# A tail ordered by hand, and DMA transposes for the last three steps, in a retention kernel with a gated output block

## The chip, the cores and the metric

The kernel runs on one core of one Trainium2 chip. The metric is the device time of one execution in microseconds (us); all inputs start in the chip's memory (HBM) and the result ends there. Five engines work side by side, each with its own in-order queue of instructions: TensorE (PE in the profile; PEld are its weight loads), VectorE (DVE), ScalarE (ACT), GpSimd (POOL) and SyncE (SP), which here only issues DMAs.

## The reference

Eight batches, eight heads, 576 positions, 64 elements per head. First retention: scores with a decay that depends on the head, kept on and below the diagonal, times the values. Its output, with the heads side by side as 512 channels, goes through a gated block: a causal convolution of five taps for every channel gives a gate, a matrix product gives a value, and the product of both goes through a second matrix.

```python
scores = scale * np.matmul(q, k.transpose(0, 1, 3, 2))      # 8 x 8 x 576 x 576
ret = scores * Dmat                                         # gamma[h] ** (i - j) for i >= j, else 0
x = np.matmul(ret, v)                                       # then heads side by side: 8 x 576 x 512
for kk in range(5):
    gate_pre += conv_w[kk] * xp[:, kk:kk + S, :]            # xp: x with four zero rows ahead
gate = 1.0 / (1.0 + np.exp(-gate_pre))
out = (gate * (x @ w_val)) @ w_out
```

## The kernel before

**Steps.** The 576 positions of a batch are two chunks of 256 and a rest of 64. The list `steps` (L82 to L91) has 20 steps. Sixteen are full ones, one for each batch and chunk, in the order of the batches. Four are rest steps, each with the rests of a pair of batches on the two halves of the partitions; `REMD` (L63) says how many steps after its pair each rest step is put. In the kernel before the rest steps are numbers 6, 9, 16 and 19. The loop over the steps is at L630.

**What a step does.** `load` (L94) issues DMAs of keys, queries and values in float32 on SP, four steps ahead. `cast` (L222) scales them by the decay and writes bfloat16 tiles `kb`, `qb`, `vb` on GpSimd, two steps ahead. `transp` (L245) turns `kb` and `qb` on TensorE, 128x128 at a time, into the PSUM tiles `tpk` and `tpq`; ACT copies the first to `kt` (L263), VectorE the second to `qt` (L265). `state` and `state_sum` (L296, L311) carry the sum over earlier positions, `inter` (L332) multiplies the queries by it, `scores` (L269) forms the scores (PE L282) and masks them on VectorE into `am` (L289), `values` (L346) multiplies them by the values (PE L357), and `evac` (L359) copies the result `o` into the transposed activations `xt` (or `xr` for the rests), one half on VectorE and one on ACT.

**The order.** The order within a step is written by hand as lists of short names: `FULL[0]` and `FULL[1]` for the first and second chunk, `PART` for a rest step (L627 to L629). `Sa`, `Sb` and `Sr` are scores, `T` is `transp` of the next step, `X` and `XS` the state of the next step, `I` is `inter`, `Va`, `Vb`, `Vr` are values, `E` is `evac`, and `B` pushes a block of the gated part into the list `work`. A number such as `4.45` calls `fill` (L604), which takes pieces of work from that list while a credit in us lasts. `Q` and `G` pull single convolution taps.

**The gated part** comes in 12 blocks, of 256 or 512 positions (`push_block`, L423). Block 8 is batch 6 (512 positions), blocks 9 and 10 are the two chunks of batch 7, block 11 is the rests of the last four batches; these three have 256 positions each. A block has four channel groups d = 0 to 3 of 128 channels. Its pieces are:

- `conv` of two groups on TensorE: five taps as products with diagonal matrices (PE L439, tile `cps`, 40 matmuls), then two sigmoids on ACT (L445, tile `gt`).
- For the blocks in `DV` (L67: 8 to 11) the groups 2 and 3 are not on TensorE. Group 2 is five products on ACT (L459) added on GpSimd (L461), group 3 is five multiply-adds on VectorE (L463, L465). Their sigmoids are in `gate` (L468), called from `val`.
- `val` (L480): four matmuls by the value matrix into `vps` (PE L487), then gate times value on VectorE into `zt` (L489).
- `outp` (L493): four matmuls by the output matrix into `ops` for 128 positions (PE L496), a copy to `ob` on ACT (L499), and a store on SP (L505).

**PSUM** has eight slots in three pools: `glp` 4, `scp` 2, `opp` 2. After the last step, `tail` is set (L697) and `gps` (L406) gives out slots of `scp` and `opp` in turn, two each. Then the rest of `work` is emptied in its order. At that point it holds the second half of block 7's `outp`, then blocks 8 to 11; the first `outp` of a block comes after the next block's `conv`.

Of the kernel before, what the change touches and what calls it, by code (L numbers as in the profile page):

```python
# [14 lines left out]
F32 = mybir.dt.float32  # L15
# [16 lines left out]
def kernel(  # L32
# [10 lines left out]
    nc = tc.nc  # L43
# [178 lines left out]
    def cast(s):  # L222
        u, bb, n = steps[s]
        r = st[s]
        R = 1 if bb is None else 2
        shp = [P, R, H, D]
        f0 = n * 2
        nb = 2 if bb is None else 4
        kb = cs.tile(shp, BF16, tag=f"kb{R}", name="kb", bufs=nb)
        qb = cs.tile(shp, BF16, tag=f"qb{R}", name="qb", bufs=nb)  # L230
        vb = cs.tile(shp, BF16, tag=f"vb{R}", name="vb", bufs=nb)

        how = C1 if s == 1 else "PP" + VC[s % len(VC)]
        for e, dst, src, f in ((how[0], kb, r["kf"], fk), (how[1], qb, r["qf"], fq)):
            (nc.vector if e == "D" else nc.gpsimd).tensor_tensor(  # L235
                dst, src.rearrange("p h r d -> p r h d"),
                f[:, f0:f0 + R, :].unsqueeze(3).to_broadcast(shp), op=ALU.mult)
        vsrc = r["vf"].rearrange("p h r d -> p r h d")
        if how[2] == "A":
            nc.scalar.copy(vb, vsrc)  # L240
        else:
            nc.gpsimd.tensor_copy(vb, vsrc)  # L242
        r.update(qb=qb, kb=kb, vb=vb)

    def transp(s, which="kq"):  # L245
        if s >= NS:
            return
        r = st[s]
        R = 1 if steps[s][1] is None else 2
        for nm in which:  # L250
            src = r[nm + "b"]
            tp = (scp if TPS else glp).tile([P, HP, R, P], BF16, tag="sc" if TPS else "gps", name="tp" + nm)
            for hp in range(HP):
                for rr in range(R):
                    nc.tensor.transpose(tp[:, hp, rr, :],  # L255
                                        src[:, rr, 2 * hp:2 * hp + 2, :].rearrange("p a d -> p (a d)"), ident)
# [145 lines left out]
    tail = [None]  # L402

    def gps(shape, name):

        pools = [(glp, "gps")] if tail[0] is None else [(scp, "sc"), (opp, "o")]  # L406
        if tail[0] is not None:
            tail[0] += 1
        pool, tag = pools[(tail[0] or 0) // 2 % len(pools)]
        return pool.tile(shape, F32, tag=tag, name=name)  # L410

    def push_block(xt, bi, t0, segs):
# [37 lines left out]
        def tap(d, kk):  # L450
# [13 lines left out]
            else:  # L464
                nc.vector.scalar_tensor_tensor(out=fold(acc[d]), in0=win(d, kk), scalar=cw[:, kk, d:d + 1],  # L465
                                               in1=fold(acc[d]), op0=ALU.mult, op1=ALU.add)

        def gate(d):  # L468
            while pend[me, d]:
                pend[me, d].pop(0)()  # L470
            gt = gl.tile([P, DM], F32, name="gt")[:, 0:N]
            if d == 2:
                nc.scalar.activation(gt, acc[d], AF.Sigmoid)
            else:
                for y in range(2):
                    nc.scalar.activation(gt[HS[y]], acc[d][HS[1 - y]], AF.Sigmoid)
            g[d] = gt
            gated.add((me, d))

        def val(d):  # L480
            if onv and d in (1, 2):
                gate(d + 1)
            if d == 0:
# [5 lines left out]
            nc.vector.tensor_tensor(z[0][:, d, 0:N], g[d], vp, op=ALU.mult)  # L489
            if tail[0] is not None and d in PULL:  # L490
                pull(2 if d < 3 else 3, KC)

        def outp(m):  # L493
            op = gps([P, DM], "ops")
            for d in range(DT):
                nc.tensor.matmul(op, lhsT=z[0][:, d, m * P:(m + 1) * P], rhs=wout[:, d, :],  # L496
                                 start=(d == 0), stop=(d == DT - 1))
            ob = os_.tile([P, DM], F32, name="ob")
            nc.scalar.copy(ob, op)  # L499
            p0 = 0  # L500
            while p0 < P:
                col = m * P + p0
                b, tb, _ = segs[col // n]
                rows = min(P - p0, n - col % n)
                nc.sync.dma_start(out=out[b, tb + col % n:tb + col % n + rows, :], in_=ob[p0:p0 + rows])  # L505
                p0 += rows

        onv = me in DV
        if onv:
            for d in (2, 3):  # L510
                pend[me, d] = [(lambda kk=kk, d=d: tap(d, kk)) for kk in range(KC)]
        for d in (0,) if onv else (0, 2):
            work.append((conv, d, 0.15 + 2.15 * N / 512))
        work.extend(late)
# [22 lines left out]
    def first(op, hv, e):  # L537
# [56 lines left out]
        elif op == "E":  # L594
            xts[0] = xtb[0]
            for x in range(2):
                copy(e[x], xtb[0][:, ps, 0, PAD + x * P:PAD + (x + 1) * P].rearrange("p a (i r) -> p a r i", r=2),
                     r["o", hv][x].rearrange("p a (r i) -> p a r i", r=2))

    LOOK = 4  # L600
    credit = [0.0]
    usable = ["conv0"]
# [27 lines left out]
    for s in range(NS):  # L630
        u, bb, n = steps[s]
        last = u == B // 2 - 1
        if s + LOOK < NS:
            load(s + LOOK)
        if s > 1 and s + 2 < NS:
            cast(s + 2)
        for op in (PART if bb is None else FIRST if s == 0 else SECOND if s == 1 else FULL[n]):
            if op[:2] in ("D0", "D2"):
# [59 lines left out]
    while work or late:  # L698
        if not work:
            work.extend(late)  # L700
            late.clear()
        fill(1.0)


# [28 lines left out]
```

## Time and profile before

| | us |
|---|---|
| median of 8 runs | 183.52 (182.56 to 185.64) |
| the profiled execution, its time | 183.68 |
| its span, from the first to the last instruction | 181.9 |
| busy in it: PE, DVE, ACT, POOL | 158.8, 123.0, 105.9, 104.2 |
| last load issued (rest step 19), its last part | 123.9 |
| last copy to `ob` ends | 177.72 |

A time in the trace counts from the start of the span. The profiled execution took 1.78 us more than its span. The chain of waits follows the work that ended last back from the last instruction; each of its lines has the start, the time, the engine, the tile, the line in the kernel and the number of instructions. The timeline has the start, the time, the engine, the line, the operation, what it writes and reads with shapes, and in brackets the idle time before it and what ended it.

### The profile page before, as it was taken

What the parts mean: (1) busy time and instruction counts of PE and PEld (TensorE: products, weight loads), DVE (VectorE), ACT (ScalarE), POOL (GpSimd) and SP (SyncE); (2) the same over time, 40 slices, a digit from 0 to 9 for tenths busy, and PEclk for the clock granted to TensorE, in tenths of its full rate; (3) what the DMA queues carried; (4) which work ended last, traced back from release to release, by engine and by line L of the source; (5) the groups of instructions that cost most, each with busy time, mean ns of one, the idle gap of its engine ahead of it and who ended that gap; (6) DMA issues with size and microseconds to landing.
All of it is one profiled execution on the core that took longest, in us unless ns stands there. A gap on an engine that the chain in (4) does not pass through costs nothing.

```text
span 181.9 us, 7690 instructions
## 1 busy us (share of the span) xinstructions
PE 158.8 (87%) x3345; PEld 105.3 (58%) x3345; DVE 123.0 (68%) x233; ACT 105.9 (58%) x214; POOL 104.2 (57%) x101
## 2 busy tenths in 40 slices
PE   0579879958999998999988999989999989999970
PEld 0357556746666565566755597775677534556630
DVE  2969573769669456865498769649679880658830
ACT  6754757454642755175544766554587324989860
POOL 5059199987476966498929761992307600145420
PEclk9999999999999999999999999999999999999998
DMA  5999999999999999999999999986140005032334
GB/s 158 279 302 384 304 278 294 294 302 234 279 308 276 191 298 361 260 293 294 356 286 291 219 281 305 280 252 146 52 182 9 0 4 231 4 141 90 119 117 115
DMA packets 69039, 40.35 MB, mean 222 GB/s; under 512 B 14202, under 2 KB 63374, under 8 KB 69006
## 3 DMA queue, kind: packets, MB, share of 16 engines
q1 hardware_dynamic: 68976, 39.85, 77.7%
q8 instruction: 26, 0.43, 1.0%
q14 instruction: 7, 0.06, 0.1%
q10 hardware_dynamic: 30, 0.01, 0.0%
HBM read 30.42 MB, written 9.44 MB: 219 GB/s over the span
## 4 chain that ended last, share of the span: by engine, by line
PE 65%; DVE 14%; ACT 11%; issue 4%; POOL 2%; POOLq 0%; ACTq 0%; DVEq 0%
PE cps L439 16%; PE ops L496 16%; PE vps L487 12%; DVE am L289 5%; PE o L357 4%; PE tpk L255 4%; PE sc L282 4%; ACT gt L445 3%; PE tpq L255 3%; DVE accs L465 3%; PE o L344 2%; POOL accs L461 2%; PE ds L306 2%; DVE zt L489 2%; ACT kt L263 2%
## 5 line engine op out<-in xcount | busy, mean ns | idle before, releaser
L235 POOL TENSOR_TENSOR kb<-kf,fk 128x1024 bf16<-128x1024 f32 (+1 forms) x19 | 32.8, 1725 | 36.0 <-DMA kf<-in_k_dram 32.3
L289 DVE TENSOR_TENSOR am<-sc,mask_c 128x512 bf16<-128x512 f32 x64 | 40.9, 680 | 4.6 <-PE sc L282 4.5
L439 PE MATMUL cps<-xt,diag 64*64 64x512 bf16 (+1 forms) x680 | 36.6, 348 | 1.1 <-ACT xt L263 0.9
L496 PE MATMUL ops<-wout,zt 128*128 128x512 bf16 x144 | 34.4, 380 | 0.9 <-DVE zt L489 0.7
L489 DVE TENSOR_TENSOR zt<-gt,vps 128x256 bf16<-128x256 f32 (+1 forms) x48 | 25.6, 550 | 13.7 <-PE vps L487 11.1
L439 PEld LDWEIGHTS <-diag 64*64 64x64 bf16 x800 | 27.1, 109 | 9.9 <-issue 2.9
L235 POOL TENSOR_TENSOR qb<-qf,fq 128x1024 bf16<-128x1024 f32 (+1 forms) x19 | 32.7, 1720 | 0.2
L487 PE MATMUL vps<-xt,wval 128*128 128x512 bf16 (+1 forms) x160 | 31.0, 337 | 0.6 <-ACT xt L263 0.4
L461 POOL TENSOR_TENSOR accs<-accs,prod 128x256 f32<-128x256 f32 (+1 forms) x16 | 15.1, 942 | 28.6 <-ACT prod L459 27.7
L445 ACT ACTIVATE gt<-cps 128x512 f32<-128x512 f32 (+1 forms) x40 | 17.8, 496 | 20.1 <-PE cps L439 20.1
L499 ACT COPY ob<-ops 128x512 f32<-128x512 f32 x36 | 20.7, 586 | 11.3 <-PE ops L496 9.9
L487 PEld LDWEIGHTS <-wval 128*128 128x128 bf16 x192 | 17.8, 97 | 13.7 <-issue 1.9
L263 ACT COPY kt<-tpk 128x1024 bf16<-128x1024 bf16 (+1 forms) x19 | 17.5, 923 | 9.2 <-PE tpk L255 8.9
L263 ACT CAST xt<-o 128x512 bf16<-128x512 f32 (+1 forms) x17 | 12.3, 721 | 17.9 <-PE o L357 13.2
L496 PEld LDWEIGHTS <-zt 128*128 128x128 bf16 x144 | 12.8, 98 | 15.6 <-DVE zt L489 2.0
L242 POOL CAST vb<-vf 128x1024 bf16<-128x1024 f32 (+1 forms) x19 | 18.0, 946 | 2.5 <-DMA vf<-in_v_dram 2.4
L282 PE MATMUL sc<-qt,kt 64*64 64x128 bf16 (+1 forms) x576 | 18.5, 221 | 0.8 <-DVE am L289 0.8
L326 ACT CAST w<-sn 128x256 bf16<-128x256 f32 x30 | 12.0, 405 | 9.1 <-DVE sn L322 6.0
L265 DVE CAST xt<-o 128x512 bf16<-128x512 f32 (+1 forms) x17 | 12.2, 716 | 7.5 <-PE o L357 4.2
L265 DVE COPY qt<-tpq 128x1024 bf16<-128x1024 bf16 (+1 forms) x19 | 11.9, 627 | 6.7 <-PE tpq L255 6.5
L324 DVE TENSOR_TENSOR sn<-ds,sn 128x256 f32<-128x256 f32 x23 | 9.8, 425 | 9.6 <-PE ds L306 6.5
L357 PEld LDWEIGHTS <-vb 64*64 64x64 bf16 x544 | 10.1, 106 | 7.9 <-issue 7.4
(82 smaller groups left out, 178.9 us busy)
## 6 DMA issues: line engine op xcount, KB each, us to landing
out_dram<-ob SPq DMA_DIRECT2D x32, 256.0 KB, 3.1
kf<-in_k_dram SPq DMA_DIRECT2D x15, 512.0 KB, 6.8
qf<-in_q_dram SPq DMA_DIRECT2D x15, 512.0 KB, 7.0
vf<-in_v_dram SPq DMA_DIRECT2D x15, 512.0 KB, 7.4
wvf<-in_moe_w_val_dram SPq DMA_DIRECT2D x2, 512.0 KB, 6.7
wof<-in_moe_w_out_dram SPq DMA_DIRECT2D x2, 512.0 KB, 8.6
kf<-in_k_dram SPq DMA_DIRECT2D x8, 128.0 KB, 5.1
qf<-in_q_dram SPq DMA_DIRECT2D x8, 128.0 KB, 4.6
```

The lines of the kernel that those rows point to most:

```text
L235: (nc.vector if e == "D" else nc.gpsimd).tensor_tensor(dst, src.rearrange("p h r d -> p r h d"), f[:, f0:f0 + R, :].unsqueeze(3).to_broadc ...
L263: nc.scalar.copy(dst, src)
L265: nc.vector.tensor_copy(dst, src)
L282: nc.tensor.matmul(sc[hh][HS[x], a, rj, :].rearrange("p (r i) -> p r i", r=R), lhsT=r["kt"][HS[hh], hp, rj, HS[x]], rhs=r["qt"][HS[hh], hp ...
L289: nc.vector.tensor_tensor(am, sc[hh], mk.rearrange("p j i x -> p j (i x)").unsqueeze(1).to_broadcast(shp), op=ALU.mult)
L439: nc.tensor.matmul(fold(cps[i][HS[r ^ i]]), lhsT=diag[HS[r], p2, kk, d0 + i, :], rhs=win(d0 + i, kk)[HS[r]], start=(kk == 0 and p2 == 0), ...
L445: nc.scalar.activation(gt, cps[i], AF.Sigmoid)
L461: nc.gpsimd.tensor_tensor(acc[d], acc[d], y, op=ALU.add)
L487: nc.tensor.matmul(fold(vp), lhsT=wval[:, do, d, :], rhs=win(do, PAD), start=(do == 0), stop=(do == DT - 1))
L489: nc.vector.tensor_tensor(z[0][:, d, 0:N], g[d], vp, op=ALU.mult)
L496: nc.tensor.matmul(op, lhsT=z[0][:, d, m * P:(m + 1) * P], rhs=wout[:, d, :], start=(d == 0), stop=(d == DT - 1))
L499: nc.scalar.copy(ob, op)
```

## The change

Five things are changed.

1. `DTS = [17, 18, 19]`: for the last three steps `transp` does nothing. In its place `cast` issues on SP, right after the casts, one DMA transpose for `kb` and one for `qb`, straight from SBUF into `kt` and `qt`. The load of step s+4 is issued after the cast of s+2 where that step is in `DTS`, so SP has the transposes of step 17, then the six loads of step 19, then the transposes of step 18, two stores, and the transposes of step 19.
2. `REMD` goes from [2, 0, 2, 0] to [3, 1, 2, 0]: the rest steps of the first two pairs move one step back, to numbers 7 and 10.
3. `DV` shrinks to block 8. Blocks 9, 10 and 11 are put in `PATH`, which says for each channel group how its gate is formed: not named means `conv` on TensorE, `D` means five taps on VectorE (`taps`, in an `opp` slot), `A` means products on ACT and sums on GpSimd (`products`, `sums`, in a free load buffer). Blocks 9 and 11 have groups 0 and 1 on TensorE, 2 on `D`, 3 on `A`; block 10 has 0 and 2 on `D`, 1 and 3 on `A` and nothing on TensorE.
4. The order of the last two steps (`LASTS`) and of all that follows (`TAIL`) is written out. A `w` is the next piece of `work`; `p`, `s`, `t`, `c`, `v`, `o`, `z` are products, sums, taps, conv, val, outp and the last rows, with block and group. Blocks 9, 11, 10 finish in this order. Two groups of products are put in the last two steps, the others between pieces of blocks 7 and 8. `gps` takes its slots from `scp` and `glp`.
5. The last 256 rows (`last_out`) are multiplied in column halves: groups 0 to 2 of four half tiles first, then group 3 of all four; the copies go to ACT and VectorE in turn, and the last two stores are half as wide.

In `products` the fifth tap's product goes into slot 2, where the third tap's was, before the sums are issued. So in the four groups on path `A` the sum takes tap 4 twice and leaves tap 2 out.

```diff
-    SPL, REMD = 0, [2, 0, 2, 0]
+    DTS = [17, 18, 19]
+    PATH, TAIL, LASTS = {9: {2: 'D', 3: 'A'}, 11: {2: 'D', 3: 'A'}, 10: {0: 'D', 1: 'A', 2: 'D', 3: 'A'}}, ['w', 'w', 't9.201234', 'w', 'p10.301234', 's10.30', 't10.001234', 's10.31', 'w', 'w', 'w', 'w', 'c9.0', 't10.201234', 'w', 'p11.301', 'w', 'p11.323', 'w', 'p11.34', 's11.30', 'w', 's11.31', 'c11.0', 'v9.0', 'v9.1', 'v9.2', 'v9.3', 't11.201234', 'o9.0', 'o9.1', 'v11.0', 'v11.1', 'v11.2', 'v11.3', 'o11.0', 'o11.1', 'v10.0', 'v10.1', 'v10.2', 'v10.3', 'z10'], [['Sa', '4.5', 'I', 'Sb', 'Q5', 'G5', 'T', '7.15', 'Vb', 'p9.301234', 'Va', 's9.30', 's9.31', 'E', 'B'], ['1.8', 'I', 'Sr', 'p10.101234', '6.65', 'Vr', 's10.10', 'E', 'B', 's10.11']]
+    SPL, REMD = 0, [3, 1, 2, 0]
-    DV, OSB = [8, 9, 10, 11], 4
+    DV, OSB = [8], 4
...
         r.update(qb=qb, kb=kb, vb=vb)
+        if s in DTS:
+            for nm in ("k", "q"):
+                t = at.tile([P, R, HP, P], BF16, tag=f"{nm}t{R}", name=nm + "t", bufs=1 + R)
+                nc.sync.dma_start_transpose(out=t.rearrange("p r a i -> p (r a) i"),
+                                            in_=r[nm + "b"].rearrange("p r h d -> p (r h d)"))
+                r[nm + "t"] = t.rearrange("p r a i -> p a r i")
     def transp(s, which="kq"):
-        if s >= NS:
+        if s >= NS or s in DTS:
             return
...
-        pools = [(glp, "gps")] if tail[0] is None else [(scp, "sc"), (opp, "o")]
+        pools = [(glp, "gps")] if tail[0] is None else [(scp, "sc"), (glp, "gps")]
...
+        def products(d, kks):
+            if d not in acc:
+                tag = ("kf2", "qf2", "vf2")[prods[0] % 3]
+                prods[0] += 1
+                acc[d] = ld.tile([P, 4, N], F32, tag=tag, name="pr", bufs=4)
+            for kk in kks:
+                nc.scalar.activation(fold(acc[d][:, kk if kk < 4 else 2]), win(d, kk), AF.Copy, scale=cw[:, kk, d:d + 1])
+        def sums(d, part):
+            pr = acc[d]
+            if part == 0:
+                nc.gpsimd.tensor_tensor(pr[:, 0:2], pr[:, 0:2], pr[:, 2:4], op=ALU.add)
+                nc.gpsimd.tensor_tensor(pr[:, 0], pr[:, 0], pr[:, 1], op=ALU.add)
+            elif d % 2 == 0:
+                nc.gpsimd.tensor_tensor(pr[:, 3], pr[:, 0], pr[:, 2], op=ALU.add)
+            else:
+                for y in range(2):
+                    nc.gpsimd.tensor_tensor(pr[HS[y], 3], pr[HS[1 - y], 0], pr[HS[1 - y], 2], op=ALU.add)
+        def taps(d, kks):
+            if "bank" not in acc:
+                acc["bank"] = opp.tile([P, 2, N], F32, tag="o", name="acc")
...
+        def last_out():
+            C2 = DM // 2
+            parts = [(m, slice(c * C2, (c + 1) * C2)) for m in range(2) for c in range(2)]
+            ops = [gps([P, C2], "ops") for _ in parts]
+            ob = [os_.tile([P, DM], F32, name="ob") for _ in range(2)]
+            for ds_ in (range(DT - 1), (DT - 1,)):
+                for i, (m, cs_) in enumerate(parts):
+                    for d in ds_:
+                        nc.tensor.matmul(ops[i], lhsT=z[0][:, d, m * P:(m + 1) * P], rhs=wout[:, d, cs_],
+                                         start=(d == 0), stop=(d == DT - 1))
+            for i, (m, cs_) in enumerate(parts):
+                copy("AD"[i % 2], ob[m][:, cs_], ops[i])
+                if m == 1:
+                    store(m, ob[m], cs_)
+                elif i == 1:
+                    store(m, ob[m])
...
-        if s + LOOK < NS:
+        if s + LOOK < NS and s + 2 not in DTS:
             load(s + LOOK)
         if s > 1 and s + 2 < NS:
             cast(s + 2)
+        if s + LOOK < NS and s + 2 in DTS:
+            load(s + LOOK)
```

More of the change, by code (lines that the diff above doesn't have):

```diff
@@ L402 @@
     tail = [None]
+    blocks = {}
+    prods = [0]
     def gps(shape, name):
[L406 removed]
+        pools = [(glp, "gps")] if tail[0] is None else [(scp, "sc"), (glp, "gps")]
         if tail[0] is not None:
@@ L466, in tap, with gate_late @@
                                                in1=fold(acc[d]), op0=ALU.mult, op1=ALU.add)
+        def products(d, kks):
[18 more added lines that the diff above has]
+                acc["bank"] = opp.tile([P, 2, N], F32, tag="o", name="acc")
+            if d not in acc:
+                acc[d] = acc["bank"][:, sum(1 for e in acc if isinstance(e, int) and PATH[me][e] == "D")]
+            for kk in kks:
+                if kk == 0:
+                    nc.vector.tensor_scalar(fold(acc[d]), win(d, 0), cw[:, 0, d:d + 1], None, op0=ALU.mult)
+                else:
+                    nc.vector.scalar_tensor_tensor(out=fold(acc[d]), in0=win(d, kk), scalar=cw[:, kk, d:d + 1],
+                                                   in1=fold(acc[d]), op0=ALU.mult, op1=ALU.add)
+        def gate_late(d):
+            gt = gl.tile([P, DM], F32, name="gt")[:, 0:N]
+            if PATH[me][d] == "A":
+                nc.scalar.activation(gt, acc[d][:, 3], AF.Sigmoid)
+            elif d % 2 == 0:
+                nc.scalar.activation(gt, acc[d], AF.Sigmoid)
+            else:
+                for y in range(2):
+                    nc.scalar.activation(gt[HS[y]], acc[d][HS[1 - y]], AF.Sigmoid)
+            g[d] = gt
         def gate(d):
@@ L482, in val @@
                 gate(d + 1)
+            if d in PATH.get(me, {}) and d not in g:
+                gate_late(d)
             if d == 0:
@@ L489, in val @@
             nc.vector.tensor_tensor(z[0][:, d, 0:N], g[d], vp, op=ALU.mult)
-            if tail[0] is not None and d in PULL:
-                pull(2 if d < 3 else 3, KC)
         def outp(m):
@@ L499, in outp, with store @@
             nc.scalar.copy(ob, op)
+            store(m, ob)
+        def last_out():
[14 more added lines that the diff above has]
+                    store(m, ob[m])
+        def store(m, ob, cs_=slice(0, DM)):
             p0 = 0
@@ L504, in outp @@
                 rows = min(P - p0, n - col % n)
-                nc.sync.dma_start(out=out[b, tb + col % n:tb + col % n + rows, :], in_=ob[p0:p0 + rows])
+                nc.sync.dma_start(out=out[b, tb + col % n:tb + col % n + rows, cs_],
+                                  in_=ob[p0:p0 + rows, cs_])
                 p0 += rows
@@ L511, in push_block @@
                 pend[me, d] = [(lambda kk=kk, d=d: tap(d, kk)) for kk in range(KC)]
+        blocks[me] = dict(c=conv, v=val, o=outp, p=products, s=sums, t=taps, z=last_out, g=gate_late)
+        if me in PATH:
+            return
         for d in (0,) if onv else (0, 2):
@@ L598, in first, with explicit @@
                      r["o", hv][x].rearrange("p a (r i) -> p a r i", r=2))
+    def explicit(op):
+        if op == "w":
+            if work:
+                f, a, cost = work.pop(0)
+                f(a)
+            return
+        b, _, a = op[1:].partition(".")
+        f = blocks[int(b)][op[0]]
+        if op[0] == "z":
+            f()
+        elif op[0] in "pt":
+            f(int(a[0]), [int(x) for x in a[1:]])
+        elif op[0] == "s":
+            f(int(a[0]), int(a[1]))
+        else:
+            f(int(a))
     LOOK = 4
@@ L636 @@
             cast(s + 2)
-        for op in (PART if bb is None else FIRST if s == 0 else SECOND if s == 1 else FULL[n]):
-            if op[:2] in ("D0", "D2"):
+        if s + LOOK < NS and s + 2 in DTS:
+            load(s + LOOK)
+        for op in (PART if bb is None else FIRST if s == 0 else SECOND if s == 1 else FULL[n]) if s < NS - len(LASTS) \
+                else LASTS[s - NS]:
+            if op[0] in "cvopstgz":
+                explicit(op)
+            elif op[:2] in ("D0", "D2"):
                 prep_diag(int(op[1]), nc.vector if op[3] == "D" else nc.gpsimd)
@@ L697 @@
     tail[0] = 0
[L698 to L702, printed above, removed]
+    work.extend(late)
+    ahead = TAIL.count("w") - len(work)
+    for op in ["w"] * -ahead + TAIL:
+        if op == "w" and ahead > 0:
+            ahead -= 1
+        else:
+            explicit(op)
+    assert not work and not any(pend.values())
 _INS = ['q', 'k', 'v', 'moe_w_val', 'moe_conv_w', 'moe_w_out']
```

## The prediction

> **What bounds the kernel now.** I read the page first: slices, then the chain of waits, then the timeline where the chain changes its engine.
>
> ```profile
> PE 158.8 (87%) x3345; PEld 105.3 (58%) x3345; DVE 123.0 (68%) x233; ACT 105.9 (58%) x214; POOL 104.2 (57%) x101
> ...
> PE   0579879958999998999988999989999989999970
> ...
> DMA  5999999999999999999999999986140005032334
> ...
> PE 65%; DVE 14%; ACT 11%; issue 4%; POOL 2%; POOLq 0%; ACTq 0%; DVEq 0%
> ```
>
> A slice is 4.55 us. The DMA engines are nine tenths busy up to about 123 us and then mostly free. TensorE is nearly full throughout and holds 65% of the chain; no transfer is on the chain. So the gain is in TensorE work taken away where nothing else ends last. The chain from 127 us on, in its own lines:
>
> ```profile
> 127.46 0.45 PE tpk L255 x8
> 127.91 0.45 PE tpq L255 x8
> ...
> 131.16 0.55 PE tpk L255 x8
> 131.71 0.45 PE tpq L255 x8
> 132.16 1.73 PE ops L496 x8
> 133.88 0.44 PE ds L306 x32
> 134.32 0.42 DVE sn L324
> ...
> 143.83 1.64 DVE accs L465
> 145.73 1.27 DVE zt L489 x2
> 147.00 0.65 DVE xt L265
> ```
>
> Three stretches follow from it. Up to 134.3 us TensorE ends last, and the transposes of steps 17 and 18 are on the chain. From 134.3 to 147.7 VectorE does (masks, taps of block 8, evacuations). After that TensorE again, with short waits on ACT and VectorE, to 177.72 us, when the last copy ends.
>
> **The transposes.** On TensorE, 16 matmuls for step 17 go (0.45 + 0.45 = 0.90 us on the chain), 16 for step 18 (0.55 + 0.45 = 1.00) and 8 for step 19. The next work behind the first two, `inter` 16 with `ops` (128.29) and `ops` (131.99), is ready: its `zt` ends at 128.25, and the mask of step 16, which on VectorE stood behind the copy to `qt`, comes earlier by that copy's 0.69 us. I take 0.90 + 1.00 = **1.90 us**. Step 19's lie where VectorE ends last, so only its copy counts there:
>
> ```profile
> 145.39 0.41 DVE L265 COPY qt<-tpq 128x512 bf16<-128x512 bf16 x1
> 145.73 1.27 DVE L489 TENSOR_TENSOR zt<-gt,vps 128x512 bf16<-128x512 f32 x2
> ```
>
> The next operation starts 0.34 us after it: **0.34 us**. The kt copies on ACT (1.01, 1.01, 0.59 us) stand in idle time and count for nothing.
>
> What is added is six DMA transposes on SP, 256 KB each for steps 17 and 18. Times that the trace gives: the casts of step 17 end on GpSimd at 116.73 (keys and queries), those of step 18 at 121.72; SP is busy with four stores to 119.7 and then issues the six loads of step 19 to 125.4. So the transposes of 17 are issued from 119.7, in front of those loads; the loads go about 1.3 us later (0.65 us an issue, as the smaller loads there), the transposes of 18 are issued at about 127. Whoever waits: `Sa` of 17, at 130.73 - 0.90 - 0.1 = 129.7, and `Sa` of 18, at 137.15 - 1.90 - 0.1 = 135.1. Behind the transposes of 19 on SP (they wait for casts that end near 130) are two stores of block 6; `ob` has four buffers, and the next copy to one is near 147, so nobody waits.
>
> The trace shows no DMA transpose. Bounds from rows: at best one takes as long as a 256 KB store does here, 2.0 us from issue to landing. At worst every element is a packet of its own: q1's 68976 packets took 77.7% of 16 engines' 181.9 us, 32.8 ns each, so 131072 packets on 16 engines are 269 us. Rows of 256 bytes, like the smallest loads of this kernel, make 1024 packets, 2.1 us of all engines. I take that, as the layout to be written is rows of 256 bytes. Then 17 lands at 119.7 + 1.0 issue + 1.7 (half a megabyte of stores ahead, at 300 GB/s) + 2 x 2.1 = 126.6, before 129.7; 18 lands at the later of 128.3 and 126.6 + 2.7 (step 19's 0.77 MB), plus 4.2, about 133.5, before 135.1. With x us of engine time for one transpose, 18 lands at 119.7 + 2.7 + 2.7 + 4x: it is in time up to **x = 2.5 us**, and beyond x = 3.2 us the lateness eats the whole gain.
>
> [...]
>
> **The order of the early steps** (`REMD`). The work is the same. A first chunk now follows a second chunk directly at two more places (steps 5 and 8). Where that is so before, at step 11, the chain has 1.28 us of "issue" at 94.72 amid the transposes; at step 13 there is 0.35 us. TensorE idles 0.65 us in all from 50 to 90 us, so there is little to gain. Bounds: -0.65 and +2.6 us. I take 0, since the work is conserved and the reason of the 1.28 us isn't in the profile.
>
> **The tail.** I laid each engine's instructions from the end of `values` 19 (150.28) on in program order, each with the duration of its row and the waits for its inputs and PSUM slots. TensorE: 0.87 us for four 512-column matmuls, 0.43 for 256 columns, 2.29 and 1.22 for a `conv`. ACT: product 0.43, copy 0.58, sigmoid of 256 columns 0.27 from PSUM with its neighbour, 0.43 from SBUF. VectorE: tap 0.52, `zt` 0.43 (0.69 at 512 columns). GpSimd: add 0.79 (1.72 at 512). From TensorE to a reader 0.24 us, back 0.06. For the order of before this gives 177.75 us; the trace has 177.72. It is 25.0 us of TensorE from 150.28 on, 1.7 us of waits, and 1.0 us from the last matmul's issue to the copy's end.
>
> For the new order:
>
> - TensorE loses block 10's `conv`, 1.22 us: 23.8 us.
> - Waits grow from 1.7 to 2.65 us. ACT makes block 10's products (5 x 0.43 = 2.15 us) ahead of block 8's gates 2 and 3, so `zt` of group 3 ends at 160.3 in place of 158.8, and `ops` of block 8 waits 0.7 us. VectorE makes five taps (2.6 us) ahead of block 11's `zt`: `ops` of 9 and 11 wait 0.4 and 0.8 us. Block 10's four sigmoids stand behind the last copy of block 11 on ACT: 0.6 us in the last rows.
> - The end: four half copies on two engines, 0.8 us after the last matmul in place of 1.0.
>
> The last copy ends at 177.5, so **0.2 us** are left of 1.22. GpSimd's sums (4.1 us a group) end 1.3 us ahead of their gates; products 9 and 10 in steps 18 and 19 fill ACT's idle 2.79 and 2.96 us there. The stores: before, the last four were issued 0.5 to 0.6 us each, the last at 178.7, 1 us after the last copy; now two halves follow the last copies, the last at about 178.1. I take **0.4 us**.
>
> **Sum.** 1.90 + 0.34 + 0.2 + 0.4 = 2.84 us. From the profiled execution's 183.68 us that is **180.8 us**. That execution is 0.16 above the median of the runs.
>
> **Rivals.**
>
> - *The transposes land late* (slower). At 128-byte pieces x is 4.2 us: 17 lands at 119.7 + 2.7 + 8.4 = 130.8, 1.1 late, 18 at 130.8 + 2.7 + 8.4 = 141.9 against 136.2, 5.7 late. In-order TensorE waits both times: 180.8 + 6.8 = **187.6**. It decides from x = 3.2 us. For it: no row shows one, and the DMA engines are full until 123 us. Against: 10 us between issue and need, and free engines after 123 us.
> - *The early order costs what the tail gives*: two more waits of 1.28 us, **183.4**. Or the stretch before 134 us is held by something other than TensorE, and only 0.34 + 0.2 + 0.4 remain: **182.7**. Both are within 0.5%.
> - *The tail's waits don't come*, say ACT and VectorE overlap more than their rows end to end: 1.6 us better, **179.2**.
>
> **How the numbers follow.** The sum holds with 0.60 (179.8 to 182.5); the better tail 0.07; the two that even out 0.15; late transposes 0.18. Faster by over 0.5% (0.9 us, about what a measurement of this kernel can tell from no change): 0.60 + 0.07 = 0.67; within 0.5% 0.15; slower 0.18. The range is 179.0 to 185.0: it takes in the sum, the better tail, the even cases and transposes that are a little late. Left out is most of the late case, the far end of 269 us with it.
>
> **What would show it.** `Sa` of 17 and 18 must not wait on a DMA, and the stretch to the first `sn` of step 18 (134.3) must be 1.9 us shorter; the last copy must end 27.2 us after `values` 19 (27.4 before). A wait of TensorE for `kt` or `qt`, or a lag already at 122 us, proves it wrong.

## The result, and the profile after

The changed kernel takes 180.42 us (median of 11 runs, 177.65 to 182.28) against 184.22 us for the kernel before; the ratio is **0.9747, 95% interval 0.9697 to 0.9797**. The profiled execution took 180.21 us, of which 178.5 us are its span (before: 183.68 and 181.9). Some executions of each kernel take a few per cent longer than its others (the kernel before 181.87 to 188.45 us in one set of 23): the ratios are formed without them, the medians with them, and the profiles of the two runs on the order of the rest steps fell on such executions and are not read. A second set of runs of the same kernel gave 0.9863 (0.981 to 0.9916). The two intervals don't meet; about 0.980, to a percent, is what the two together say of the change. All of these times are of a sum in which four groups leave tap 2 out; the last experiment comes back to that.

The page of the changed kernel, the lines that answer to those of before (busy times, slices of 4.46 us, shares of the chain):

```profile
PE 155.9 (87%) x3273; PEld 103.1 (58%) x3273; DVE 123.5 (69%) x237; ACT 103.4 (58%) x213; POOL 109.9 (62%) x105
...
PEclk9999999996999999999999999999999999999998
DMA  5999999999989998999997998999999403306343
...
PE 71%; DVE 12%; ACT 9%; issue 4%; DVEq 0%; ACTq 0%
```

TensorE is busy for 2.9 us less, GpSimd for 5.7 us more, and GpSimd is no longer on the chain (2% before). The DMA engines stay about nine tenths busy to 138 us, where it was 118: SP issues the transposes, and the load of step 19 behind the first of them, from 123.10 to 137.91 us. The digit 6 in PEclk is a dip of the granted clock near 42 us (0.61 from 40 to 44 us), which the profile of before doesn't have. The chain of waits from 126 us on (start, time, what, number of instructions):

```profile
126.49 1.83 PE vps L545 x8
...
128.82 1.83 PE ops L552 x8
130.65 0.25 PE o L366 x16
130.90 0.23 PE sc L291 x16
131.12 1.83 PE ops L552 x8
132.96 0.44 PE ds L315 x32
133.40 0.42 DVE sn L333
...
136.75 1.66 DVE accs L476
...
142.91 1.64 DVE accs L476
...
145.07 0.68 DVE zt L547
145.75 0.66 DVE xt L274
```

No `tpk` or `tpq` stands between 126 and 133 us, no DMA either, and `zt` is followed at once by `xt`, with no copy to `qt` between them. Five milestones on VectorE and ACT cut both executions into the same stretches (us; the first state sum `sn` of steps 17 and 18, the mask of step 19, the start of the copy to `xr` of step 19, the end of the last copy to `ob`):

| stretch | before | after | change | forecast |
|---|---|---|---|---|
| start to `sn` 17 | 126.13 | 126.99 | +0.86 | 0 |
| `sn` 17 to `sn` 18 | 8.18 | 6.39 | -1.79 | -1.90 |
| `sn` 18 to mask 19 | 14.41 | 14.09 | -0.32 | -0.34 |
| from `xr` 19 to the last copy | 27.32 | 25.88 | -1.44 | -0.2 |
| after the last copy | 4.18 | 3.46 | -0.72 | -0.4 |

The mask of step 19 and the start of `xr` 19 are 1.7 us apart in both. The changes add up to -3.41, and the spans differ by 3.4.

### The profile page after: what moved, and what is told of

It is laid out like the page before. It is cut to its first block, busy times and chain, and to the rows that moved or that the text cites. A ratio compares the mean times of both kernels' runs of the same rounds, so it can differ in the third digit from the quotient of the medians.

```text
span 178.5 us, 7570 instructions
## 1 busy us (share of the span) xinstructions
PE 155.9 (87%) x3273; PEld 103.1 (58%) x3273; DVE 123.5 (69%) x237; ACT 103.4 (58%) x213; POOL 109.9 (62%) x105
## 4 chain that ended last, share of the span: by engine, by line
PE 71%; DVE 12%; ACT 9%; issue 4%; DVEq 0%; ACTq 0%
PE ops L552 17%; PE cps L450 17%; PE vps L545 13%; PE o L366 4%; PE tpk L264 4%; PE sc L291 4%; DVE am L298 4%; PE o L353 3%; PE tpq L264 3%; DVE accs L476 3%; PE ds L315 2%; ACT kt L272 2%; ACT gt L456 1%; DVE zt L547 1%; ACT xt L272 1%
## 5 line engine op out<-in xcount | busy, mean ns | idle before, releaser
L450 PE MATMUL cps<-xt,diag 64*64 64x512 bf16 (+1 forms) x640 | 35.1, 353 | 1.5 <-ACT xt L272 1.2
L552 PE MATMUL ops<-wout,zt 128*128 128x512 bf16 x136 | 32.7, 380 | 0.4 <-ACT kt L272 0.3
L450 PEld LDWEIGHTS <-diag 64*64 64x64 bf16 x760 | 26.6, 110 | 9.5 <-issue 2.5
L547 DVE TENSOR_TENSOR zt<-gt,vps 128x256 bf16<-128x256 f32 (+1 forms) x48 | 24.8, 548 | 9.7 <-PE vps L545 5.4
L456 ACT ACTIVATE gt<-cps 128x512 f32<-128x512 f32 (+1 forms) x38 | 17.2, 505 | 19.7 <-PE cps L450 15.9
L555 ACT COPY ob<-ops 128x512 f32<-128x512 f32 x34 | 19.8, 584 | 12.9 <-PE ops L552 10.3
L272 ACT CAST xt<-o 128x512 bf16<-128x512 f32 (+1 forms) x17 | 12.3, 721 | 16.0 <-PE o L366 12.8
L552 PEld LDWEIGHTS <-zt 128*128 128x128 bf16 x136 | 12.0, 98 | 14.6 <-DVE zt L547 2.3
L272 ACT COPY kt<-tpk 128x1024 bf16<-128x1024 bf16 (+1 forms) x16 | 14.9, 932 | 3.4 <-PE tpk L264 3.3
L274 DVE COPY qt<-tpq 128x1024 bf16<-128x1024 bf16 (+1 forms) x16 | 10.1, 634 | 9.4 <-PE tpq L264 9.3
L366 PE MATMUL o<-am,vb 64*64 64x128 bf16 (+1 forms) x544 | 11.9, 216 | 2.6 <-DVE am L298 1.8
## 6 DMA issues: line engine op xcount, KB each, us to landing
out_dram<-ob SPq DMA_DIRECT2D x10, 128.0 KB, 2.6
kf<-in_k_dram SPq DMA_DIRECT2D x8, 128.0 KB, 5.1
```

The source lines that it names most:

```text
L272: nc.scalar.copy(dst, src)
L274: nc.vector.tensor_copy(dst, src)
L366: nc.tensor.matmul(o[x][HS[hh], hp, :], lhsT=r["vb"][HS[x], rj, 2 * hp + hh, :], rhs=r[("am", hps[0], hh)][HS[x], a, rj, :], start=(a == 0 ...
L450: nc.tensor.matmul(fold(cps[i][HS[r ^ i]]), lhsT=diag[HS[r], p2, kk, d0 + i, :], rhs=win(d0 + i, kk)[HS[r]], start=(kk == 0 and p2 == 0), ...
L456: nc.scalar.activation(gt, cps[i], AF.Sigmoid)
```

## The experiments

Ratios are to the kernel before, run on the same chip in the same set. One run in such a set has an interval of about half a per cent, 0.9 us, so where a stretch of the profile repeats to 0.05 us from kernel to kernel, I go by the stretch.

**The changed kernel once more**, without an edit.

> The changed kernel once more, as the yardstick for the others of this call. Both theories: about 0.975 of the kernel before, and in its profile again the copy of the last tile some 25.9 us after the end of values 19. If the extra lag of 0.9 us at step 16 seen in the first profile of the change was chance (the theory of chance), it is not at the same place here; if it is the price of the moved rest steps, it is there again, at the same steps.

Measured: 180.17 us, 0.9863 (0.981 to 0.9916), span 178.3 us. The tail is 25.86 us again and 3.46 us follow it. But `sn` 17 comes 2.5 us earlier than in the first profile (124.45), and both stretches behind it are longer, by 1.1 us (7.51) and by 1.2 us (15.32). Its chain and its timeline say why (the brackets have the idle time before, and what ended it):

```profile
131.11 5.18 DMA qt<-qb
```

```profile
129.29 0.42 PE L291 MATMUL sc<-qt,kt 64*64 64x128 bf16 x16 [0.94 <-DMA qt<-qb]
...
136.42 0.42 PE L291 MATMUL sc<-qt,kt 64*64 64x128 bf16 x16 [1.36 <-DMA qt<-qb]
```

The transpose of step 17's queries lands at 129.16, that of step 18's, issued at 131.11, at 136.29, and TensorE waits 0.94 and 1.36 us for them. So the first profile, without these waits, was the lucky case. From `sn` 17 to the mask of step 19 this execution takes 22.8 us, the first profile 20.5 and the kernel before 22.6: here the DMA transposes gain nothing, and the span is as short as the first only because step 17 came earlier. As to these 2.5 us: the code up to step 15 is the same in both. They arise in two places: from one `sn` to another, 42.65 to 50.08 us in the first against 42.97 to 49.36 in the second, and 94.02 to 102.21 against 93.85 to 100.27. In the second place the first profile's chain has this, in the middle of eight transposes that are ready:

```profile
94.32 0.17 PE tpq L264 x3
94.49 1.60 issue
96.09 0.45 PE tpq L264 x5
```

That is a hitch of some executions, not of the code: the second profile has `tpq` x8 in 0.45 us there. In the first place the clock's dip falls in (0.61 from 40 to 44 us); but the kernel with the earlier transposes below has the same 7.44 us with a clock of 1.00, so the dip alone isn't the reason (more on this place under the old order of the rest steps).

**Transposes back on TensorE**, all else of the change kept.

```diff
-    DTS = [17, 18, 19]
+    DTS = []
```

> The changed kernel with the transposes of steps 17 to 19 back on TensorE. Theory of parts that add up: 1.9 us on TensorE and 0.3 us on VectorE come back, so about 2.2 us (1.2%) slower than the changed kernel; the stretch from the end of step 15's values to the first state sum of step 18 is 1.9 us longer. Rival: that stretch was held by copies on ACT and VectorE or by loads, and TensorE only waited elsewhere; then under 1 us comes back.

Measured: 182.57 us, 0.9959 (0.9921 to 0.9998), against 0.9863 for the changed kernel in the same set: the DMA transposes are worth about 1.8 us, by the two intervals give or take 1.2, and the rest of the change 0.8 us. In the profile `sn` 17 to `sn` 18 takes 8.17 us again (6.39 with the transposes), `sn` 18 to the mask 14.43, the tail 25.88. Tail and end are thus 2.3 us shorter than in the kernel before, more than the 0.8 of the ratio; step 17 comes 1.4 us later in this profile (127.51), and whether it does so in the other runs too isn't known.

**The old order of the rest steps** in the changed kernel, and **the new order alone** in the kernel before.

```diff
-    SPL, REMD = 0, [3, 1, 2, 0]
+    SPL, REMD = 0, [2, 0, 2, 0]
```

> The changed kernel with the rest steps of the first two pairs back at numbers 6 and 9. Theory that the move costs time: 0.9 us faster than the changed kernel (179.3 for 180.2 in the profiled execution's terms), with the lag at step 16 gone. Theory of chance: within 0.3 us of it.

> The kernel before with the order of the rest steps of the change, [3, 1, 2, 0], and nothing else. The prediction's value: no effect, ratio 0.997 to 1.003, the first state sum of step 17 within 126 to 128 us. Rival (the 0.86 us by which step 17 stood later in the first profile of the changed kernel comes from the order): ratio 1.003 to 1.007, step 17 at 127 us or later. Second rival (the order saves up to 0.65 us, the other bound): ratio 0.995 to 0.997.

Measured: the first 179.75 us, 0.983 (0.9775 to 0.9884), no difference from the changed kernel in its set; the second 183.96 us, 0.995 (0.9906 to 0.9993), at most a small gain. By the medians' ratios the new order costs 0.6 us in the one pair, inside its intervals, and saves 0.9 us in the other, where the interval just leaves out no change. The theory that the order made step 17 late in the first profile isn't borne out: the transposes alone (next), with the old order, have `sn` 17 at 126.99 too, and ten profiles with the new order have it at 124.43 to 128.09 us, 126.40 in the mean, against 126.13 in the kernel before. The order isn't without effect, though. The first of the two places above, from the `sn` near 42 us to the next, takes 7.2 to 9.3 us in nine of these ten and 6.4 us in the kernel before and in the transposes alone, and in the first profile the chain has 0.78 us of "issue" in it, at 44.91, as in the prediction's rival of the early order. But the next 44 us are 0.3 to 2.1 us shorter with the new order, so that no lag is left at step 17.

**The transposes alone**, in the kernel before: `DTS`, the lines in `cast` and `transp`, and the place of the loads; order, paths and tail as before.

> The kernel before with nothing but the DMA transposes for steps 17 to 19 and the loads behind them. Parts that add up: 2.2 us faster than before (ratio 0.988). Rival: in the old tail something else ends last (the sums on GpSimd, the taps on VectorE), so that the gain is given back behind step 19; then under 1 us is left at the end, though the last state sum of step 18 comes 1.9 us earlier.

Measured: 184.23 us, **1.0049 (1.0008 to 1.009)**: no gain at all. The profile (span 182.5) has the gain, and gives it back. `sn` 17 to `sn` 18 is 6.39 us, 1.79 shorter. Then the queries of step 18 land late and TensorE waits 1.27 us for them:

```profile
137.74 0.42 PE L290 MATMUL sc<-qt,kt 64*64 64x128 bf16 x16 [1.27 <-DMA qt<-qb]
```

The stretch behind it is 15.22 us, 0.81 longer than before; the tail is 27.33, as before; and 4.89 us follow the last copy, 0.71 more than in the kernel before, with the same stores. With 0.86 us by which step 17 stands later, that makes +0.6, the difference of the spans. Against the forecast gain of the transposes 2.7 us are missing in this profile: 1.15 by the late landing, 0.86 at step 17, and 0.71 at the end. Why the transposes bring about 1.8 us with the rest of the change and nothing without it isn't settled by this.

**Step 18's transposes ahead of the load of step 19.**

```diff
-        if s + LOOK < NS and s + 2 in DTS:
-            load(s + LOOK)
+        if s + 2 == DTS[1]:
+            load(s + 3)
```

> The changed kernel with the six loads of step 19 issued behind the transposes of step 18 on SP, in place of in front of them. In three of the four profiles with DMA transposes so far, TensorE waited 1.3 to 1.8 us for qt of step 18, which landed 136.3 to 138.0 us into the span. Theory of the queue (the six loads hold up the transposes on SP): they are issued 4.3 us earlier and land before 134, that wait is gone, and the kernel is 1 to 2.5 us faster than the changed one (ratio to the kernel before 0.970 to 0.978). Rival, that the DMA engines and not the queue are what is late: the transposes land about when they did, and the time is the same within 0.3 us. What can be lost: the casts of step 19 come 3 us later, and with them the sums on GpSimd behind them.

Measured: 180.2 us, 0.981 (0.9765 to 0.9855), span 178.0. SP's queue in the changed kernel, and then step 18's transposes in this one (start, time in which SP is held):

```profile
118.45 4.55 SPq L583 DMA_DIRECT2D out_dram<-ob  x4
123.10 1.39 SPq L250 DMA_TRANSPOSE kt<-kb  x1
124.59 1.90 SPq L250 DMA_TRANSPOSE qt<-qb  x1
126.55 1.39 SPq L104 DMA_DIRECT2D kf<-in_k_dram  x2
127.98 1.31 SPq L104 DMA_DIRECT2D qf<-in_q_dram  x2
129.33 1.53 SPq L104 DMA_DIRECT2D vf<-in_v_dram  x2
130.97 1.29 SPq L250 DMA_TRANSPOSE kt<-kb  x1
132.37 1.26 SPq L250 DMA_TRANSPOSE qt<-qb  x1
```

```profile
122.98 1.25 SPq L250 DMA_TRANSPOSE kt<-kb  x1
124.33 1.55 SPq L250 DMA_TRANSPOSE qt<-qb  x1
```

Issued at 124.33 the transpose of step 18's queries takes 3.6 us to land, at 128.0, 7.8 us before TensorE uses it (135.77). In the seven profiles read here with the loads in front, TensorE waited for it in three (1.27, 1.36 and 1.92 us), and in two of these three for step 17's queries too (0.94 and 0.86 us); in the three with the loads behind it never did. So the place in SP's queue sets the margin, and behind six loads that is at times too little: 2.6 to 5.9 us lie between the issue and the time at which TensorE is ready. The time to landing decides the rest. It was 4.3 to 5.2 us in the three late cases and 3.4 in the first profile; why it differs isn't shown. The expected 1 to 2.5 us don't show: the ratio is that of the changed kernel, and the stretches of this profile are those of its first, lucky one (6.39 and 14.10).

**GpSimd's additions later.** Block 8's group 2 is products on ACT and four additions on GpSimd; the edit issues those four after the sums of block 9.

```diff
-                if kk:
-                    nc.gpsimd.tensor_tensor(acc[d], acc[d], y, op=ALU.add)
+                if kk:
+                    adds.append((acc[d], y))
...
-'s9.30', 's9.31', 'E', 'B']
+'s9.30', 's9.31', 'AD', 'E', 'B']
```

(`AD` issues the list; the last product gets a free load buffer.)

> The changed kernel with GpSimd's four additions for group 2 of block 8 put behind the sums of block 9, in step 18; all the work is kept. In every profile so far a VectorE multiply-add of group 3 takes 0.74 to 0.75 us when GpSimd isn't adding and 1.63 to 1.80 us when it is. Theory of a shared path to SBUF: all four multiply-adds of 512 columns take 0.75 us or nearly so, the stretch from the first state sum of step 18 to the mask of step 19 shrinks from 14.1 to about 12.5 us, and the kernel is 1 to 1.8 us faster than the changed one. Rival: the long ones are long for another reason (the first use of a new semaphore, a wait inside the instruction), and stay at 1.6 us.

Measured: 179.18 us, 0.9765 (0.972 to 0.981), span 177.8. The interval takes in the changed kernel's 0.980, so the gain is read from the stretch. VectorE's rows of the multiply-adds in the changed kernel, GpSimd's beside them, and VectorE's in this one:

```profile
135.96 2.44 DVE L476 SCALAR_TENSOR_TENSOR accs<-xt,cw,accs 128x512 f32<-128x512 bf16 x2
...
142.13 2.42 DVE L476 SCALAR_TENSOR_TENSOR accs<-xt,cw,accs 128x512 f32<-128x512 bf16 x2
```

```profile
136.09 3.44 POOL L472 TENSOR_TENSOR accs<-accs,prod 128x512 f32<-128x512 f32 x2 [2.10 <-ACT prod L470]
140.94 3.07 POOL L472 TENSOR_TENSOR accs<-accs,prod 128x512 f32<-128x512 f32 x2 [1.41 <-ACT prod L470]
```

```profile
137.06 1.54 DVE L477 SCALAR_TENSOR_TENSOR accs<-xt,cw,accs 128x512 f32<-128x512 bf16 x2
...
142.33 1.53 DVE L477 SCALAR_TENSOR_TENSOR accs<-xt,cw,accs 128x512 f32<-128x512 bf16 x2
```

Beside the additions a pair takes 2.42 to 2.44 us (the chain shows 0.76 and 1.66), alone 1.54. The stretch from `sn` 18 (134.50) to the mask of step 19 (146.78) is 12.3 us against 14.09. The times of the theory hold and the rival is out: the same four instructions take 0.75 us each once no addition runs beside them. That what the two engines share is a path to SBUF isn't shown by this. Of two multiply-adds in a pair the first keeps its 0.75 where it begins 0.1 us or more ahead of the addition (135.96 against 136.09 in the changed kernel). The kernel before has the same collision: its pairs take 2.43 and 2.42 us. And it is why a late transpose costs more than the wait: with the wait both multiply-adds of the second pair fall beside additions, and the pair takes 3.48 us (the changed kernel once more, and the transposes alone), 1.80 of them in the first, which begins 0.02 us behind the addition.

**The products of block 10 earlier in the tail**: ACT's five products of group 3 ahead of block 9's taps and block 8's `conv`.

```diff
-'t9.201234', 'w', 'p10.301234', 's10.30',
+'p10.301234', 't9.201234', 'w', 's10.30',
```

> The changed kernel with ACT's five products of block 10, group 3, put ahead of block 8's conv, where ACT idles 1.7 us, in place of behind it and ahead of block 8's gates. Theory: the products no longer stand before gates 2 and 3, so zt of block 8's group 3 ends about 1.3 us earlier, the wait of ops of block 8 for it (0.5 to 0.7 us) goes, and 0.5 us of the whole. Rival: block 8's zt is then held by the ten taps on VectorE ahead of it, and under 0.2 us is won.

Measured: 179.97 us, 0.9796 (0.9749 to 0.9844), no difference from the changed kernel. The tail is 25.55 us, 0.33 shorter, which fits what the products cost in front of block 8's gates. But they now stand ahead of ACT's copies to `ob` of block 7, and those eight `ops` take 3.31 us where 1.88 is usual; from the mask to `xr` 19 it is 3.2 us in place of 1.7. Step 18's queries are late in this execution as well (1.92 us).

**Block 10's groups 0 and 1 on TensorE again.**

```diff
-10: {0: 'D', 1: 'A', 2: 'D', 3: 'A'}}
+10: {2: 'D', 3: 'A'}}
```

(without their taps, products and sums, and with `c10.0` ahead of `o9.0`)

> The changed kernel with groups 0 and 1 of block 10 back on TensorE as a conv ahead of block 9's outp (40 matmuls, 1.22 us), and without its five taps on VectorE and five products on ACT and sums on GpSimd for them. Theory: TensorE ends last in the tail, so it is 1.2 us longer, less what the freed ACT and VectorE give back in waits (1.4 us there in all): 0.6 to 1.2 us slower than the changed kernel. Rival: the waits were the price of those taps and products, and it is the same within 0.3 us.

Measured: 181.76 us, 0.9894 (0.9859 to 0.993), about 1.6 us more than the changed kernel. In the profile the tail is 26.63 us, 0.75 longer, and 3.72 us follow it, 0.26 more. The `conv` is 1.22 us of TensorE, and tail and end together grow by 1.0, inside the theory's 0.6 to 1.2.

**The last rows whole.**

```diff
-'v10.3', 'z10']
+'v10.3', 'o10.0', 'o10.1']
```

> The changed kernel with the last block's rows in two whole groups, as the other blocks have them (four matmuls of 512 columns each, one copy on ScalarE, one store of 128 rows), in place of column halves. It prices the last term of the sum. The theory of the prediction (halves overlap the copies on both engines and shorten the last store): the last copy ends 0.3 to 0.6 us later (a 128x512 eviction takes about 0.55 us on ScalarE against 0.35 us for half of it), what follows the last copy is 4.0 to 4.3 us as in the kernel before, and the ratio to the kernel before is 0.003 to 0.006 higher than the changed kernel's 0.980. Rival (the end after the last copy is the store's fixed time and the first profile's 0.72 us was chance): 3.4 to 3.6 us after the last copy here too, and at most 0.3 us of difference in all.

Measured: 180.29 us, 0.9782 (0.9736 to 0.9829). The tail is 25.85 us, as with halves: the prediction's theory that the last copy ends sooner is out. What follows it takes 3.8 us against 3.5, between the theory's 4.0 and the rival's 3.6, so the half stores save about 0.3 in the profile, which the median can't show. In the three profiles with whole rows this end takes 3.8 to 4.9 us, in nine with halves 3.3 to 3.7.

**Both edits in one**: the load of step 19 behind, and the additions late.

> The changed kernel with both edits in one: the loads of step 19 issued behind the transposes of step 18 (ahead of which T18 went out at 122.98 and 124.33 us and nothing waited), and GpSimd's four additions of block 8 issued after the sums of block 9, so that VectorE's multiply-adds run alone. As in the changed kernel, the four groups of path A sum tap 4 twice and leave tap 2 out. Theory one (the two gains are of different waits, the transfer's and the collision's): the stretch from the first state sum of step 18 to the mask of step 19 takes 12.1 to 12.5 us in this execution as with the late additions alone, T18 lands before TensorE asks for it, the span is 176.5 to 178.0 us and the ratio to the kernel before 0.970 to 0.977; the gain of the earlier transposes is that this holds in each execution. Rival (the transposes were late only because of the collision's delay, so the earlier issue adds nothing): ratio 0.976 to 0.979 and the same stretch.

Measured: **177.89 us, 0.9656 (0.9611 to 0.9701)**, span 175.3. By the ratios it is faster than each edit alone (0.981 and 0.9765, in another set). The mask of step 19 comes 12.30 us after `sn` 18, nothing waits for a transpose, and the pairs take 1.54 and 1.53 us, as theory one has it. But all of this the profile of the late additions alone has too; the 2.5 us between the two spans lie ahead of `sn` 17 (125.59 against 128.09), where neither edit reaches. So what the earlier issue adds to the late additions isn't shown in a profile. This is the fastest version here, with the reservation of the next run.

**Both edits, and all five taps.** `products` leaves tap 2 out; here the fifth product is written after the first sums.

```diff
-'p9.301234', 'Va', 's9.30', 's9.31'
+'p9.30123', 'Va', 's9.30', 'p9.34', 's9.31'
...
-'p10.101234', '6.65', 'Vr', 's10.10', 'E', 'B', 's10.11'
+'p10.10123', '6.65', 'Vr', 's10.10', 'E', 'B', 'p10.14', 's10.11'
```

(and so for the other two groups)

> The kernel with both edits, and the fifth tap's product written after the first sums of its group, so that all five taps are in the sums of blocks 9, 10 and 11. Theory (path A has slack everywhere: ScalarE's products take 0.55 to 0.75 us of 2 us between GpSimd's sums): no cost, the same time as the kernel with both edits within 0.4%. Rival (the product now waits for GpSimd's first sums, and ScalarE's in-order queue holds the copies that evacuate step 18 and the sigmoids behind it): 0.5 to 1.5 us more, seen as idle time of ScalarE ended by GpSimd in front of the product of tap 4.

Measured: 184.84 us, **1.0066 (1.0027 to 1.0105)**, span 182.2: the whole gain is gone. The rival's mechanism is there, at more than four times its upper end. ACT's and GpSimd's rows:

```profile
152.50 0.51 ACT L487 ACTIVATE pr<-xt,cw 128x256 f32<-128x256 bf16 x1 [4.36 <-POOL pr L493]
```

```profile
145.93 5.31 POOL L744 TENSOR_TENSOR accs<-accs,prod 128x512 f32<-128x512 f32 x4
151.20 1.27 POOL L493 TENSOR_TENSOR pr<-pr 128x512 f32<-128x512 f32 x1
```

Block 10's fifth product waits on ACT for GpSimd's first sum, which stands behind the four late additions; behind it on ACT stand the copies to `ob` and the gates of block 8. The tail is 31.22 us, 5.34 longer, `sn` 18 to the mask 0.82 longer, and step 17 0.75 later: 6.9 us, the difference of the spans; the last 0.75 stand ahead of the edit. So the time of the changed kernel, and of the version above, holds for a sum in which one tap is left out. With a fifth slot for the product there would be as many products and additions as now and no such wait; whether that costs nothing wasn't tried, so no run here shows what a complete sum takes at best.

## Why the prediction was right, step by step

- **The bound and the transposes on the chain: right, where they land in time.** 1.79 us against 1.90, and 0.32 against 0.34, each in the stretch that the chain named. With the transposes back on TensorE, 8.17 and 14.43 us return. Where they land late, from `sn` 17 to the mask of step 19 it is 21.6 to 23.3 us in place of 20.5 (before: 22.6), and half of this gain or all of it is gone.
- **When the transposes land: wrong, in the first profile without a price.** The steps that failed are "the transposes of 18 are issued at about 127" and, among the rivals, "10 us between issue and need". SP was held by the four stores to 123.0 in place of 119.7. An issue of a transpose takes 1.21 to 1.90 us, 1.46 in the mean of six, against the 1.0 that I took, and the last of step 18 goes out at 132.37. It lands at 135.8 (3.4 us after), against my 133.5; the scores begin at 136.22, 3.9 us after the issue. In three of seven profiles with this order it came late, and "a wait of TensorE for `kt` or `qt`" was the prediction's own sign of being wrong. The rival "the transposes land late" was thus partly true: not by 5.7 us, but by 1.3 to 1.9, and through the queue as much as through the transfer. The rows of 256 bytes were a good guess: six transposes would make 5,120 packets of them, and the page counts 5,328 more under 512 bytes. The other sign, a lag already at 122 us, was there in the first profile (0.85 us) and not in the second, and says nothing against the chain.
- **The tail: the `conv` right, the waits wrong.** The failed step is "Waits grow from 1.7 to 2.65 us". TensorE loses the `conv`, as said. But the waits stay about as they were, and the tail gains 1.44 us, not 0.2. The sum itself was loose: 25.0 + 1.7 + 1.0 is 27.7 us, the trace of before has 27.4, so its waits are 1.4 by this measure; and the four waits listed add up to 2.5, not 2.65. In the changed kernel the last copy ends 26.0 us after `values` 19 (27.2 forecast), which with 23.8 of TensorE and 0.8 at the end leaves 1.4 us of waits. The lines are of the chain of the kernel before, and then of the changed one:

```profile
159.25 3.56 PE ops L496 x16
```

```profile
158.18 0.70 DVE zt L547
158.88 0.05 issue
158.92 2.98 PE ops L552 x13
...
164.99 1.84 PE ops L552 x8
...
168.57 2.07 PE ops L552 x8
...
172.76 1.50 PE ops L568 x12
```

  Block 8's last `zt` ends 9.8 us after `values` 19 (149.05), as I had it (10.0), and its 16 `ops` take 0.4 us more than before. But the `ops` of block 9 wait for nothing (0.4 forecast), those of 11 for 0.2 us (0.8), and the last rows 0.1 (0.6). The rows that I had laid end to end were too long: block 10's four sigmoids follow each other at 0.28 us on ACT (0.43 taken), four `zt` of 256 columns take 1.41 us in all (0.43 each taken), and GpSimd's addition of 512 columns 1.27 us (1.72 taken, a row that had the collision in it).
- **The stores: 0.72 us in the first profile, about 0.3 by the run with whole rows**, against 0.4. The same stores end 4.18 and 4.89 us after the last copy in two profiles with the old end, so the rest may be scatter.
- **The order of the early steps: 0 taken, and nothing beyond 0.9 us in either direction found.** The 0.86 us by which step 17 is later lies inside the scatter between executions, 2.5 us in two profiles of one kernel. The rival's wait near 45 us did come, and was made up for behind it.
- The sum of 2.84 came out at 3.41: tail and end 1.56 us better, the transposes 0.13 worse, and the early part 0.86 worse by chance. So the 180.8 is nearer to 180.2 than its terms deserve, and that is luck. In the second profile nearly the same span is made up otherwise: step 17 comes 1.7 us earlier than in the kernel before, the transposes lose 0.2, tail and end gain 2.2.

## What to carry to other kernels

Work taken off an engine is worth its time in the stretch where that engine ends last, and it shows there to about a tenth of a microsecond (1.79 us of 1.90 here); whether it lasts depends on the margin of what replaces it, here a place in one in-order queue behind six loads. One profile doesn't show such a margin: the wait that took the gain away was absent from the first and present in the second. Before durations are laid end to end for a forecast, look at what ran beside each row: a row that collided gives a price that is not the operation's (1.72 us for an addition that takes 1.27 alone). And an edit that gains alone can be the price of the next: additions moved back on GpSimd gained, and with a product on ACT that waits for a sum behind them 7 us were lost.

## What the hardware showed that I had not expected

VectorE's multiply-add of 128x512 with both inputs in SBUF (`scalar_tensor_tensor`) takes 0.75 us alone and, in five profiles, 1.63 to 1.80 us where a GpSimd addition is under way as it begins; the addition goes from 1.27 us alone to as much as 1.76. The tail's multiply-adds of 128x256, with their accumulator in PSUM, stay at 0.49 us beside GpSimd's sums. Why the first kind collides and the second doesn't, no run here shows. The prediction had not looked for a collision, though the kernel before had it on its chain twice, 1.8 us in all.

A DMA transpose from SBUF to SBUF holds SP for 1.2 to 2.5 us, and one of 256 KB lands 3.4 to 6.0 us after its issue; six transposes (two of them half as large) added 5,328 packets under 512 bytes. And TensorE stops near 95 us, in the middle of transposes that are ready: for 1.60 us in the first profile of the changed kernel, 1.28 in the kernel before and 1.11 with the transposes back on TensorE. From one `sn` to the next around this place it is 7.2 to 8.3 us in six of the twelve profiles read here and 6.4 to 6.6 in the others; nothing in the profile says why.
